# Loading the keys of one batch quad as one large transfer and sixteen small ones

## The chip, the cores and the metric

The kernel runs on one core of a Trainium2 chip. A core has five engines that run their own instruction streams: TensorE (PE in the profile, with its weight loads as PEld), VectorE (DVE), ScalarE (ACT), GpSimd (POOL) and SyncE (SP), which here does nothing but start transfers. The transfers between the chip's main memory (HBM) and the on-chip memory (SBUF, 128 partitions) are carried out by 16 DMA engines that all queues of the core share. The metric is device time of one execution in microseconds (us), the lower the better.

## The reference

One decoding step of attention with grouped heads over a sliding window, with the projections before and after it:

```
x: (32, 1, 512)   k_cache, v_cache: (32, 8, 2048, 128)   wq: (512, 4096)   wo: (4096, 512)    all bf16
W = 512                                   # only the last 512 of 2048 positions are used
q = (x @ wq), as 32 batches x 32 heads x 128
k, v = the last W positions of the caches; 4 query heads share one of the 8 key/value heads
p = softmax(q . k / sqrt(128))            # over the 512 positions
out = (p . v), as 32 x 4096, @ wo         # 32 x 1 x 512
```

The window of K is 32 x 8 x 512 x 128 numbers of two bytes, 32 MiB in all, and that of V as much. Each weight matrix has 4 MiB. So some 75.5 MB must be read for rather little arithmetic.

## The kernel before, in words

The 32 batches are worked off in eight *quads* of four batches. For a quad, the 4 x 8 pairs of batch and key head, times four blocks of 128 positions each, make the 128 partitions: partition p holds pair p // 4 and block p % 4, and its row is 128 positions of 128 numbers, 32 KB (the function `rows` makes this view of the cache). A quad of K or of V is so 4 MiB. K has two buffers, `K_sb[0]` and `K_sb[1]`, and V two more; quads take turns on them.

For quad q, VectorE turns K in two halves (step T, `turn`, L439 to L441: a transpose of 32 x 32 blocks), TensorE makes scores (S), VectorE takes maxima (M), ScalarE the exponentials (X), VectorE divides by the sums (N), TensorE moves the probabilities to the partitions of V (E), ScalarE copies them out (G), ScalarE and VectorE spread them to a block-diagonal form (B), TensorE multiplies with V (P, L361), both engines pick the blocks that count from the result (C), and TensorE and ScalarE fold them into the operand of the last product (F, D). After all quads TensorE multiplies with `wo` (L390), VectorE and ScalarE copy the result out, and one DMA writes it.

The order on each engine is written out by hand in the strings `PE_OPS`, `DVE_OPS` and `ACT_OPS`; nothing is rescheduled. What an operation waits for is worked out from the table in `needs`. VectorE's order around the middle is

```
... M3 N3 B3.0.4 T4.0 T4.1 M4 N4 B4.0.4 T5.0 C3.2.3 T5.1 C3.3.4 T6.0 M5 T6.1 ...
```

All loads of K, V and `wo` are issued by SyncE, in the order of the list `LOADS`:

```
K0 K1 V0.0 K2 V1.0 K3 V2.0 K4 V3.0 K5 K6 V4.0 K7 V5.0 V5.1 V6.0 V6.1 V7.0 V7.1 V7.2 V7.3 W0 W1 W2
```

Before K of quad q is issued, SyncE waits until the second half of T of quad q - 2 is done, which frees the buffer; before V of quad q it waits for the last product of quad q - 2 with V. The three parts of `wo` go into `K_sb[0]` behind T of quad 6. K of a quad is one DMA (L228). It adds 16 to the semaphore of its buffer when all of it has landed, and `turn` waits for 16 times the number of loads that this buffer has had. The last quads of V come in two, two and four pieces with semaphores of their own.

The input `x` (32 rows of 1 KB) is loaded first, by ScalarE's queue, in four DMAs of 2, 6, 10 and 14 rows. In the trace, SyncE's transfers are queue q1, ScalarE's are q10; q8 and q14, "instruction", are transfers that fetch the engines' own instructions through the same 16 DMA engines.

Of the kernel before, what the change touches and what calls it, by code (L numbers as in the profile page):

```python
# [38 lines left out]
X_PARTS = [(0, 2), (2, 8), (8, 18), (18, 32)]  # L39
V_PIECES = [1, 1, 1, 1, 1, 2, 2, 4]  # L40
WOP = [(0, 16), (16, 28), (28, 32)]


def ops_of(text):
    return [(w[0],) + tuple(int(n) for n in w[1:].split(".")) for w in text.split()]


def bass_standalone__sliding_block_cached__sampling_kernel(
# [7 lines left out]
):  # L56
    B, Sq, D = x.shape
    _, HKV, SK, DH = k_cache.shape
    HD = wq.shape[1]
    HQ = HD // DH  # L60
# [7 lines left out]
    KB = 4  # L68
    R = W // KB
# [50 lines left out]
    with ExitStack() as es:  # L120
# [3 lines left out]
        K_sb = [sb(f"K_sb{i}", [P, R * DH], BF16) for i in range(2)]  # L124
# [42 lines left out]
        sem_k = [sem(f"sem_k{i}") for i in range(2)]  # L167
        sem_v = [[sem(f"sem_v{i}_{j}") for j in range(max(V_PIECES))] for i in range(2)]
        sem_wo = [sem(f"sem_wo{i}") for i in range(len(WOP))]
        sem_out = sem("sem_out")  # L170
# [20 lines left out]
        def load_wq(i):  # L191

            nc.sync.dma_start(
                wq_sb[:, 2 * i:2 * i + 2, :].rearrange("p k n -> p (k n)"),
                wq.rearrange("(p k) n -> p k n", k=DKT)[:, 2 * i:2 * i + 2].rearrange("p k n -> p (k n)"),
            ).then_inc(sem_wq[i], 16)
# [4 lines left out]
        def rows(cache, q, r0=0, r1=R):  # L201
            return cache[4 * q:4 * q + 4, :, SK - W:, :].rearrange(
                "b h (k r) d -> (b h) k (r d)", k=KB)[:, :, r0 * DH:r1 * DH]
# [14 lines left out]
        @block.sync  # L218
        def _(sp):
            wait = Waits(sp)  # L220
            load_wq(1)
            wo_r = wo.rearrange("(p i) n -> p i n", i=NI)
            for op in ops_of(" ".join(LOADS)):
                kind, q = op[0], op[1]
                if kind == "K":
                    if q >= 2:
                        wait([ends["T", q - 2, 1]])
                    sp.dma_start(K_sb[q % 2][:, :], rows(k_cache, q)).then_inc(sem_k[q % 2], 16)  # L228
                elif kind == "V":
                    if q == 1:  # L230
                        sp.wait_ge(s["pe_q"], 8)
                    if q >= 2:
                        wait([ends["P", q - 2, 31]])
                    n = R // V_PIECES[q]
                    r0 = op[2] * n
                    sp.dma_start(  # L236
                        V_sb[q % 2][:, r0 * DH:(r0 + n) * DH], rows(v_cache, q, r0, r0 + n)
                    ).then_inc(sem_v[q % 2][op[2]], 16)
                else:
                    wait([ends["T", NQ - 2, 1]])  # L240
                    i0, i1 = WOP[q]
                    sp.dma_start(  # L242
                        wo_sb[:, i0:i1, :].rearrange("p i n -> p (i n)"),
                        wo_r[:, i0:i1, :].rearrange("p i n -> p (i n)"),
                    ).then_inc(sem_wo[q], 16)
            sp.wait_ge(s["dve_y"], 2)
            sp.wait_ge(s["act_y"], 2)
            sp.dma_start(
                out.rearrange("b s n -> b (s n)"), out_sb[:, :, :].rearrange("b c n -> b (c n)")
            ).then_inc(sem_out, 16)  # L250
            sp.wait_ge(sem_out, 16)
# [44 lines left out]
        def _(pe):  # L296
# [88 lines left out]
            wait([ends["D", NQ - 1]])  # L385
            for j, (i0, i1) in enumerate(WOP):
                pe.wait_ge(sem_wo[j], 16)
# [10 lines left out]
        def spread_args(q, h):  # L398
            return bd[:, q % 2, :, h, :], PTc[:, q % NG], mask[:, h:h + 1]

        def pick_args(q, r):
            pr = slice(32 * r, 32 * r + 32)
            return C_sb[pr, q % 2], O_ps[pr, :, r * DH:(r + 1) * DH]

        @block.vector
        def _(dve):
            wait = Waits(dve)
            dve.wait_ge(s["pe_xT"], 1)
            dve.tensor_copy(  # L409
                xT_sb[:, :, :].rearrange("p k c -> p (k c)"), Y_ps  # L410
            ).then_inc(s["dve_xT"], 1)
            dve.wait_ge(s["pool_f"], 2)
            dve.tensor_reduce(
                F_hd[:, :], F_id[:, :, :].rearrange("p r h -> p h r"), AX.X, ALU.add
            ).then_inc(s["dve_c"], 1)
            dve.wait_ge(s["pool_m"], 2)
            dve.tensor_reduce(
                m_red[:, :].rearrange("p (h k) -> p h k", h=HKV),
                m_id[:, :, :, :].rearrange("p b h k -> p h k b"), AX.X, ALU.add,
            ).then_inc(s["dve_c"], 1)  # L420
            dve.wait_ge(s["dve_c"], 2)
            dve.wait_ge(s["pool_fz"], 1)
            dve.tensor_reduce(
                mask[:, :], m_red[:, :].rearrange("p (h k) -> p h k", h=HKV), AX.X, ALU.add
            ).then_inc(s["dve_c"], 1)
            for d in range(4):
                dve.tensor_copy(F_sb[:, d, :, d], F_hd[:, :]).then_inc(s["dve_c"], 1)
            for n in range(4):
                dve.wait_ge(s["pe_q"], 2 * n + 1)
                dve.tensor_copy(Q_row[:, 1024 * n:1024 * n + 512], ps[:, 2 * n]).then_inc(s["dve_q"], 1)  # L430
            dve.wait_ge(s["dve_q"], 4)
            dve.wait_ge(s["act_q"], 4)
            dve.transpose(  # L433
                QT_sb[:, :, :, :, :].bitcast(F32).rearrange("p j w h t -> p h w (j t)"),
                Q_row.bitcast(F32).rearrange("p (h w c) -> p h w c", h=HQ, w=2),
            ).then_inc(s["dve_QT"], 1)
            dve.wait_ge(s["dve_QT"], 1)

            def turn(q, w):  # L439
                dve.wait_ge(sem_k[q % 2], 16 * (q // 2 + 1))  # L440
                return dve.transpose(  # L441
                    KT_sb[:, w].bitcast(F32).rearrange("p r c t -> p r (c t)"),
                    K_sb[q % 2][:, :].bitcast(F32).rearrange("p (r w c) -> p r w c", r=R, w=2)[:, :, w],
                )

            def maxes(q):
                dve.tensor_reduce(maxv[:, q:q + 1], S_ps, AX.X, ALU.max).then_inc(s["dve_m"], 1)  # L447
                dve.wait_ge(s["dve_m"], q + 1)
                return dve.tensor_scalar(  # L449
                    negmax[:, q:q + 1], maxv[:, q:q + 1], -SCALE, None, op0=ALU.mult)  # L450

            def norm(q):
                dve.reciprocal(recip[:, q:q + 1], sums[:, q:q + 1]).then_inc(s["dve_r"], 1)
                dve.wait_ge(s["dve_r"], q + 1)
                return dve.tensor_scalar(  # L455
                    P_bf[:, :], P_f32[:, :], recip[:, q:q + 1], None, op0=ALU.mult)

            def spread(q, h0, h1):
                for h in range(h0, h1):
                    o, i, m = spread_args(q, h)  # L460
                    ins = dve.tensor_scalar(o, i, m, None, op0=ALU.mult)  # L461
                return ins

            def pick(q, r0, r1):
                for r in range(r0, r1):
                    ins = dve.tensor_copy(*pick_args(q, r))  # L466
                return ins

            run = {"T": turn, "M": maxes, "N": norm, "B": spread, "C": pick}
            for op in orders["DVE"]:  # L470
                wait(needs(op))
                run[op[0]](*op[1:]).then_inc(op_sem["DVE", op[0]], 1)
            dve.wait_ge(s["pe_Y"], 1)
            for c in range(2):
                dve.tensor_copy(
                    out_sb[:, c, :], Y_ps[32 * c:32 * (c + 1), 0:P]
                ).then_inc(s["dve_y"], 1)
# [77 lines left out]
```

## Time and profile before

| | us |
|---|---|
| median of three runs (186.52 to 186.93) | 186.64 |
| the profiled execution, its own time | 186.46 |
| its span, from the first to the last instruction | 184.7 |
| SyncE issues K of quad 4 | 61.97 |
| SyncE issues V of quad 3, the next in its list | 71.66 |
| VectorE starts T of quad 4, having waited for the DMA | 92.22 |
| the last piece of `wo` has landed | 181.60 |

The span is 1.76 us shorter than the execution's own time. Busy shares of the five engines are 65% at most (TensorE), while the DMA engines are busy in nearly every slice of the span but the first and the last; over the span they read 75.53 MB at a mean of 409 GB/s. Times inside the execution are counted from the start of the span. Where the chain of waits names a DMA, its duration runs from the start of the issuing instruction to the landing, so it includes the time in which the DMA stands in the queue behind earlier ones.

The trace also keeps every single packet of a DMA (a row of 32 KB is one packet) with its start, duration, size and queue, and the time of every increment that a DMA engine makes to a semaphore. It doesn't name the DMA engine.

### The profile page before, as it was taken

The page shows a single profiled execution, that of the slowest core. Times are in us where ns is not written, and L with a number is a line of the kernel's source. Part 1 is how long each engine was busy: PE and PEld are TensorE (multiplying, and loading weights), DVE is VectorE, ACT ScalarE, POOL GpSimd, SP SyncE. Part 2 cuts the span into 40 slices and gives each one's busy share as a digit, 9 for nine tenths or more (in the row PEclk, how much of TensorE's full clock was granted, in tenths as well). Part 3 has the DMA queues.
Part 4 walks back from the last instruction along what each step waited for, and adds up shares of the span by engine and source line. Part 5 has one row for each costly group of instructions (what it writes and reads, how often), then busy time and mean ns, then how long its engine had stood idle before and what let it go on. Part 6 is the DMA issues. An engine that isn't in the chain of part 4 may idle for free.

```text
span 184.7 us, 3664 instructions
## 1 busy us (share of the span) xinstructions
PE 120.1 (65%) x1636; PEld 56.9 (31%) x1636; DVE 106.5 (58%) x106; ACT 49.8 (27%) x93; POOL 16.9 (9%) x52
## 2 busy tenths in 40 slices
PE   0089304436599795749944992441899799898942
PEld 0024100013344451403521350000345345354541
DVE  0030999996469632963298327999746996311201
ACT  3000400010952357101650162001072804511211
POOL 7900040201000100002000200010000000000000
PEclk9999955555879999555999699555589999999998
DMA  6999999999999999999999999999999999999970
GB/s 220 411 497 405 405 454 454 447 397 405 451 454 451 390 401 454 454 444 405 392 451 454 440 397 412 454 433 440 415 412 422 419 429 426 410 419 433 425 305 31
DMA packets 3872, 75.80 MB, mean 410 GB/s; under 512 B 464, under 2 KB 528, under 8 KB 656
## 3 DMA queue, kind: packets, MB, share of 16 engines
q1 hardware_dynamic: 3792, 75.53, 96.1%
q8 instruction: 13, 0.21, 0.5%
q10 hardware_dynamic: 64, 0.03, 0.1%
q14 instruction: 3, 0.02, 0.0%
HBM read 75.53 MB, written 0.03 MB: 409 GB/s over the span
## 4 chain that ended last, share of the span: by engine, by line
DMA 59%; DVE 22%; PE 10%; issue 6%; SPq 2%; ACTq 1%; DVEq 0%
DMA K_sb<-in_k_cache_dram 43%; DVE KT_sb L441 16%; DMA K_sb<-in_wo_dram 12%; PE ps L313 4%; PE ps L361 4%; DMA bd<-in_x_dram 4%; DVE QT_sb L433 2%; DVE KT_sb L430 1%; SPq L236 1%; DVE C_sb L466 1%; ACTq L187 1%; SPq L242 1%; PE ps L331 1%; DVE bd L409 0%; PE ps L301 0%
## 5 line engine op out<-in xcount | busy, mean ns | idle before, releaser
L441 DVE STREAM_TRANSPOSE KT_sb<-K_sb 128x4096 f32<-128x4096 f32 x16 | 70.5, 4430 | 10.5 <-DMA K_sb<-in_k_cache_dram 10.4
L361 PE MATMUL ps<-V_sb,bd 32*128 32x512 bf16 x1024 | 63.9, 401 | 4.2 <-DMA V_sb<-in_v_cache_dram 1.6
L331 PE MATMUL ps<-KT_sb,QBD 128*32 128x512 bf16 x256 | 25.1, 529 | 37.3 <-DVE KT_sb L441 28.1
L361 PEld LDWEIGHTS ps<-V_sb,bd 32*128 32x128 bf16 x1024 | 27.3, 98 | 38.5 <-issue 14.9
L331 PEld LDWEIGHTS ps<-KT_sb,QBD 128*32 128x32 bf16 x256 | 6.6, 113 | 52.7 <-DVE KT_sb L441 34.1
L492 ACT ACTIVATE P_f<-ps,negmax 128x512 f32<-128x512 f32 x8 | 5.5, 685 | 60.6 <-DVE negmax L449 60.6
L505 ACT ACTIVATE bd<-PTc,mask 128x512 bf16<-128x512 bf16 x31 | 20.1, 710 | 0.3
L510 ACT ACTIVATE C_sb<-ps 32x512 f32<-32x512 f32 x22 | 12.9, 588 | 25.2 <-PE ps L361 25.1
L289 POOL COPY QBD<-QT_sb 32x128 bf16<-32x128 bf16 x32 | 9.2, 287 | 106.8 <-PE ps L331 89.2
L461 DVE TENSOR_SCALAR bd<-PTc,mask 128x512 bf16<-128x512 bf16 x33 | 9.4, 349 | 14.2 <-ACT PTc L499 14.2
L466 DVE COPY C_sb<-ps 32x512 f32<-32x512 f32 x10 | 6.9, 693 | 14.5 <-PE ps L361 14.3
L373 PE MATMUL ps<-C_sb,F_sb 128*128 128x128 f32 x64 | 10.1, 306 | 7.1 <-ACT C_sb L510 6.5
L373 PEld LDWEIGHTS ps<-C_sb,F_sb 128*128 128x128 f32 x64 | 8.6, 208 | 10.0 <-ACT C_sb L510 8.7
L346 PE MATMUL ps<-P_bf,E_sb 128*128 128x128 bf16 x128 | 10.1, 243 | 0.8 <-DVE P_bf L455 0.8
L313 PE MATMUL ps<-V_sb,bd 128*128 128x512 bf16 x32 | 9.8, 480 | 0.8 <-DVE bd L409 0.8
L346 PEld LDWEIGHTS ps<-P_bf,E_sb 128*128 128x128 bf16 x128 | 8.6, 110 | 4.9 <-DVE P_bf L455 2.8
L447 DVE TENSOR_REDUCE maxv<-ps 128x1 f32<-128x512 f32 x8 | 5.5, 687 | 7.8 <-PE ps L331 7.7
L499 ACT ACTIVATE PTc<-ps 128x512 bf16<-128x512 f32 x8 | 4.8, 594 | 18.5 <-PE ps L346 18.4
L430 DVE CAST KT_sb<-ps 128x512 bf16<-128x512 f32 x4 | 2.5, 684 | 7.3 <-PE ps L313 7.3
L301 PE MATMUL ps<-bd 32*128 32x128 bf16 x4 | 0.6, 295 | 9.0 <-DMA bd<-in_x_dram 9.0
L409 DVE CAST bd<-ps 128x512 bf16<-128x512 f32 x1 | 0.7, 691 | 9.6 <-PE ps L301 9.6
L486 ACT ACTIVATE KT_sb<-ps 128x512 bf16<-128x512 f32 x4 | 2.1, 602 | 15.1 <-PE ps L313 15.1
(29 smaller groups left out, 34.1 us busy)
## 6 DMA issues: line engine op xcount, KB each, us to landing
K_sb<-in_k_cache_dram SPq DMA_DIRECT2D x8, 4096.0 KB, 25.4
V_sb<-in_v_cache_dram SPq DMA_DIRECT2D x5, 4096.0 KB, 29.6
V_sb<-in_v_cache_dram SPq DMA_DIRECT2D x4, 2048.0 KB, 20.5
V_sb<-in_wq_dram SPq DMA_DIRECT2D x2, 2048.0 KB, 9.8
V_sb<-in_v_cache_dram SPq DMA_DIRECT2D x4, 1024.0 KB, 11.6
K_sb<-in_wo_dram SPq DMA_DIRECT2D x1, 2048.0 KB, 18.6
K_sb<-in_wo_dram SPq DMA_DIRECT2D x1, 1536.0 KB, 21.7
K_sb<-in_wo_dram SPq DMA_DIRECT2D x1, 512.0 KB, 22.4
```

Source lines behind the costliest of these rows:

```text
L289: pool.tensor_copy(QBD[pr, q % 2].rearrange("p (w t) (h c) -> p w t h c", w=2, h=HKV)[:, :, :, :, 4 * b:4 * b + 4], QT_sb[pr, q].rearrange ...
L313: ins = pe.matmul(ps[:, n], lhsT=xT_sb[:, kt, :], rhs=wq_sb[:, kt, n * 512:(n + 1) * 512], start=kt == 0, stop=kt == DKT - 1, tile_positio ...
L331: ins = pe.matmul(S_ps[32 * c:32 * c + 32, :], lhsT=QBD[:, q % 2, 2 * w + t, c0:c0 + 32], rhs=KT_sb[:, w, :, KB * h:KB * h + KB, t], start ...
L346: ins = pe.matmul(EP_ps[:, e * R:(e + 1) * R], lhsT=E_sb[:, k, e].rearrange("p m j -> p (m j)"), rhs=P_bf[:, k * R:(k + 1) * R], start=k = ...
L361: ins = pe.matmul(O_ps[:, b, :], lhsT=bd[pr, q % 2, 4 * g:4 * g + 4].rearrange("p r h e -> p (r h e)"), rhs=V_sb[q % 2][pr, 512 * g:512 * ...
L373: ins = pe.matmul(F_ps[:, 0:P], lhsT=F_sb[:, d].rearrange("p h d -> p (h d)"), rhs=C_sb[:, q % 2, :, 32 * d:32 * d + 32], start=d == 0, st ...
L441: return dve.transpose(KT_sb[:, w].bitcast(F32).rearrange("p r c t -> p r (c t)"), K_sb[q % 2][:, :].bitcast(F32).rearrange("p (r w c) -> ...
L447: dve.tensor_reduce(maxv[:, q:q + 1], S_ps, AX.X, ALU.max).then_inc(s["dve_m"], 1)
L461: ins = dve.tensor_scalar(o, i, m, None, op0=ALU.mult)
L466: ins = dve.tensor_copy(*pick_args(q, r))
L505: ins = act.activation(o, i, ACTF.Copy, scale=m)
L510: ins = act.activation(*pick_args(q, r), ACTF.Copy)
```

## The change

Quad 4 of K, and that quad alone, is no longer one DMA of 128 rows of 32 KB. One DMA brings the first 28 KB of each of the 128 rows. The last 4 KB of the rows come by 16 further DMAs of eight partitions each: for each group of 32 neighbouring partitions and each k of 0 to 3 the partitions 32 g + k, 32 g + k + 4, ..., 32 g + k + 28, in the order g = 0, k = 0 to 3, then g = 1 and so on. Each of the 17 DMAs adds 16 to the same semaphore, so VectorE waits for 16 x 19 increments ahead of T of quad 4 and for 16 x 20 ahead of T of quad 6. All else, the bytes and their places included, is as before.

```diff
+K_SPLIT = (4,)
+K_TAIL = 2048
...
-                    sp.dma_start(K_sb[q % 2][:, :], rows(k_cache, q)).then_inc(sem_k[q % 2], 16)
+                    k_rows = rows(k_cache, q)
+                    n = R * DH - (K_TAIL if q in K_SPLIT else 0)
+                    sp.dma_start(
+                        K_sb[q % 2][:, :n], k_rows[:, :, :n]
+                    ).then_inc(sem_k[q % 2], 16)
+                    if q in K_SPLIT:
+
+                        for p0 in [32 * g + k for g in range(4) for k in range(KB)]:
+                            sp.dma_start(
+                                K_sb[q % 2][p0:p0 + 29:4, n:],
+                                k_rows[p0 // 4:p0 // 4 + 8, p0 % 4, n:],
+                            ).then_inc(sem_k[q % 2], 16)
...
-                dve.wait_ge(sem_k[q % 2], 16 * (q // 2 + 1))
+                dve.wait_ge(sem_k[q % 2], 16 * sum(17 if p in K_SPLIT else 1 for p in range(q % 2, q + 1, 2)))
```

## The prediction

> **What bounds the kernel now.** I read the page's DMA rows first.
>
> ```profile
> DMA  6999999999999999999999999999999999999970
> ...
> DMA packets 3872, 75.80 MB, mean 410 GB/s; under 512 B 464, under 2 KB 528, under 8 KB 656
> ...
> q1 hardware_dynamic: 3792, 75.53, 96.1%
> q8 instruction: 13, 0.21, 0.5%
> q10 hardware_dynamic: 64, 0.03, 0.1%
> q14 instruction: 3, 0.02, 0.0%
> ```
>
> The 16 DMA engines never run dry between the first and the last slice. The chain of waits then shows that the end hangs on them.
>
> ```profile
> 159.19 22.41 DMA K_sb<-in_wo_dram
> 181.60 0.04 issue
> 181.64 0.44 PE ps L390 x16
> 182.08 0.02 issue
> 182.10 0.28 DVE P_bf L475
> ```
>
> The last piece of `wo` lands at 181.60; behind it come 16 matmuls, the copy-out and the store, 3.07 us to the end of the span at 184.67. So the time is: when does the last DMA engine finish its share of all loads? K of quad 4 itself has much room, as two timelines show (SyncE, then VectorE):
>
> ```profile
> 61.97 0.54 SPq L228 DMA_DIRECT2D K_sb<-in_k_cache_dram  x1
> 71.66 0.54 SPq L236 DMA_DIRECT2D V_sb<-in_v_cache_dram  x1
> 81.59 19.96 SPq L228 DMA_DIRECT2D K_sb<-in_k_cache_dram  x2
> 101.59 0.60 SPq L236 DMA_DIRECT2D V_sb<-in_v_cache_dram  x1
> ```
>
> ```profile
> 92.22 8.77 DVE L441 STREAM_TRANSPOSE KT_sb<-K_sb 128x4096 f32<-128x4096 f32 x2 [1.16 <-DMA K_sb<-in_k_cache_dram]
> ```
>
> Issued at 61.97, it lands at 92.19, behind 20 us of older loads.
>
> The DMA engines don't end together. The increments of the 16 engines for the last piece of `wo`, in order of time:
>
> ```
> 178.32 178.38 178.42 178.51 178.62 | 179.11 179.16 179.57 | 179.87 179.94 180.15 180.20 | 181.33 181.41 181.44 181.60
> ```
>
> Packets of one engine follow each other within 3 to 4 ns, so the records can be strung into 16 chains. The 12 instruction fetches of 16 KB (q8) ahead of the end sit on eight chains: one each for the first eight, and the ninth to twelfth on the chains of the first four. Each costs its engine about 1.1 to 1.6 us (at 81.56 fetch and 32 KB packet together took 2.77 instead of 1.21). Three fetches of 8 KB (q14) sit on three other chains. So the groups above are five engines without a fetch, three with an 8 KB one, four with one of 16 KB, and four with two.
>
> **The change, part by part.**
>
> *Issue.* 16 more DMAs on SyncE at 0.53 to 0.62 each (its rows) are at most 9.9 us. Starting at 62.51 they end by 72.4, and V of quad 3, free at 71.66, goes out 0.7 later at most. Its data can't move before K of quad 4 is through at about 90: 18 us of cover, cost nothing. K of quad 5 waits until 81.59 anyway.
>
> *Which engines carry the tail.* The four loads of `x` (2, 6, 10 and 14 rows) left 64 packets on q10: 32 rows and 32 completions, one for each row, while SyncE's 27 loads wrote 432 completions of 4 B, 16 each. So a DMA of eight rows should run on eight engines, one row each, and all 16 tails on the same eight if each begins at the same engine. (The Trainium skill, "DMA: Bandwidth & Descriptors", section "Why a DMA increments its semaphore by 16 and not by 1", says that HWDGE takes the lowest-numbered k engines; the packet counts agree with k, but no row here gives an engine's number.) Which eight: the chains with most `x` rows should be the first engines. The first two fetches of q8 fall on chains with two `x` rows, the third and sixth on chains with one, the q14 fetches on chains with three or four, the eighth seems to fall on one with three. Mostly, then, the q8 fetches are on the engines that get no tail. I put 9 in 10 on that.
>
> *Work per engine.* Periods from packet to packet: 32 KB 1.213, 16 KB 0.610, 4 KB 0.155, a completion 0.006. On the line between, 28 KB takes 1.06. Before, quad 4 of K costs each engine 8 x 1.213 + 0.006 = 9.71. After:
> - an engine without tail: 8 x 1.06 + 0.01 = 8.49, so -1.22;
> - an engine with tail: 8.49 + 16 x (0.155 + 0.006) = 11.07, so +1.36.
>
> The queues stay full, so both shifts last until the end. The four latest would land at 181.60 - 1.22 = 180.38. The eight with tail, now 178.32 to 179.57, would land at up to 179.57 + 1.36 = 180.93. By this alone the end moves by -0.67.
>
> *Two streams to the same partitions.* Half of the tail, 32 KB on each of eight engines, belongs to rows that the other eight brought before, and these go on with V meanwhile. If the way into SBUF goes with the partitions, two streams share one there; no row shows 32 KB of that. Lower bound 0: the 1 KB packets of `x` took 46 ns each beside full streams, and the streams' 16 KB packets stayed at 0.611. Upper bound, equal sharing at an unchanged sum: the 32 KB take twice 1.21, so +1.21 for an engine with tail, and +1.21 for its partner, whose gain is gone. The nearest row for several engines at neighbouring partitions is the store of the output, 16 engines on 32 neighbours: 13 of its 32 packets of 1 KB took 65 to 79 ns instead of 46, up to 1.7 times. A buffer can swallow 1 KB of `x`, but not 32 KB, so I take the full 1.21.
>
> The Trainium skill, "SBUF — State Buffer", section "Door 1: The DMA port swizzle", says that DMA bandwidth depends on how many of 16 ports the partitions reach, and that partitions 64 apart are on different ports. Its map would put all rows that change engines on the other eight's ports. By this rule the sum is the one below; were engines alone the limit, it would be the -0.67 above.
>
> *Sum.* Engines with tail: 179.57 + 1.36 + 1.21 = 182.14 for the latest. The others: 181.60 - 1.22 + 1.21 = 181.59. The end moves from 181.60 to 182.14, +0.54.
>
> *The added wait.* VectorE's wait for quad 4 now ends with the tail: engines that landed at 90.47 to 90.91 land by 93.5, the one with a q14 fetch at 90.27 by about 94. T of quad 4 starts 1.3 to 1.9 late; behind it in VectorE's order stand M4, N4, B4, and the scores of quad 4, K of quad 6 and V of quad 4 wait for that. K of quad 6, due at 101.0, can't move before K of quad 5 ends at 109.9: hidden. K of quad 5 and of quad 7 land later by the same shift (140.92 to 140.28 + 2.57 = 142.85 for quad 7), and so T of quad 7, the picks behind it, and the issue of V of quad 7 at 155.5 by 1.9. Packets follow an issue by about 1.0 (first `wq` issue 0.73, packet 1.755), so at 158.4; the first engine without work would be one at 160.06 less 0.45 from packet to increment. Cover 1.2, cost nothing. The last products with V end at 174.2, up to 1.0 later; the `wo` product then starts by 178.4 and waits for its second part at 180.9: hidden.
>
> The sum is against the profiled execution: 186.46 + 0.54 = 187.00. That execution lies 0.18 under the median of the runs, 186.64, so I forecast 187.2.
>
> **Rivals.**
>
> *Faster: nothing is shared.* The engines with tail end at 180.93 and the late ones at 180.38: 186.64 - 0.67 = 185.97. For it: the untouched 0.611 beside `x`. Against it: those bursts are 1 KB. It decides as long as sharing costs less than 0.67 on the latest engine with tail, since 0.67 is what the balance gives.
>
> *No change that can be measured.* Sharing costs about half (0.3 to 1.0, the end within 0.37 of before), or the tails spread over all 16 engines. In the latter case each gets 8 packets of 4 KB in place of part of its rows: 8.49 + 8 x 0.161 = 9.78, +0.07: 186.7. Against even spreading: the completion counts of `x`.
>
> *Slower by more: the tail falls on the engines with the q8 fetches.* 181.60 + 1.36 = 182.96, or 184.17 with sharing: 188.0 to 189.2. For it speaks the eighth fetch, against it the first three and the sixth.
>
> *Slower by issue.* It would need SyncE to hold up V of quad 3 by 18 us, over 1.6 for each small DMA; its rows say 0.6. I give it no chance of its own.
>
> **How the numbers follow.** What this measurement can tell from no change is about 0.2%, 0.37 us. Forecast 0.46 (slower); faster rival 0.33; no change 0.13; tail on the late engines 0.08 (slower). Hence faster 0.33, same 0.13, slower 0.54. The forecast's own range is 186.9 to 187.7: below by a milder sharing, above by sharing that loses some of the sum. The range for 8 in 10 must take in the faster rival, 185.97, and leaves out the tail on the late engines: 185.7 to 187.7.
>
> **What would show it.**
> - Issue: SyncE's rows of L239, 16 of about 0.6, and V of quad 3 at about 72.
> - Engines: 128 data packets more and, on eight engines each, 16 x 8 = 128 completions: q1 should have 4048 packets; on 16 engines each it would have 4176.
> - Work: the 4 KB packets of the tail at 0.155 for one half; with sharing, the other half near 0.31 and V's 32 KB packets beside them above 1.213.
> - K of quad 4 at T's start: about 93.5 to 94 with sharing, 92.3 to 93 without.
> - The end: last increments for `wo` in two groups, with sharing the engines with tail last at 182.1, without at 180.9.
>
> Wrong if V's packets keep their 1.213 next to the tail, or if the late groups of the last piece of `wo` move up instead of down.

## The result, and the profile after

The changed kernel took 190.31 us, the median of six runs (188.08 to 191.0), against 186.75 of the kernel before, run beside it (186.52 to 187.39). The ratio is 1.014, with a 95% interval of 1.0098 to 1.0182; it is not the quotient of the medians, which is 1.019, and it leaves out the run at 191.0, which counts as a slow one. The forecast of 187.2 had the right sign, and the time lies far outside its range of 185.7 to 187.7.

The six times are not one cloud: 188.08 and 188.28, then 190.22, 190.40, 190.72 and 191.0. The kernel before shows no such gap. So there are two questions: what costs some 1.5 us in an execution at 188, and what costs 2.4 more in one at 190.5. The profiled execution is one of the first kind, 188.08; it took 1.62 longer than the profiled one of before, and its span of 186.3 is longer by as much. Three more profiles, shown further below, are of the second kind.

The page's DMA rows of the changed kernel, in the order in which the prediction showed those of before:

```profile
DMA  6999899999899999999999999999999999999980
...
DMA packets 4128, 75.80 MB, mean 407 GB/s; under 512 B 592, under 2 KB 656, under 8 KB 912
...
q1 hardware_dynamic: 4048, 75.53, 96.2%
q8 instruction: 13, 0.21, 0.5%
```

The bytes are the same, the engines are as busy, and yet the mean rate is 407 instead of 410 GB/s: the same work takes the engines longer. The 4048 packets of q1 are exactly the number that the prediction gave for tails that run on eight engines.

SyncE's timeline of the changed kernel (start, duration, engine, line, operation):

```profile
62.05 0.53 SPq L233 DMA_DIRECT2D K_sb<-in_k_cache_dram  x1
62.62 10.82 SPq L239 DMA_DIRECT2D K_sb<-in_k_cache_dram  x16
73.49 0.60 SPq L250 DMA_DIRECT2D V_sb<-in_v_cache_dram  x1
81.49 23.28 SPq L233 DMA_DIRECT2D K_sb<-in_k_cache_dram  x2
```

The 16 issues cost 0.68 each. V of quad 3 goes out 1.83 later than before, and its data still has nowhere to go until K of quad 4 is through, at about 89.

VectorE's timeline at T of quad 4 and the second half of T of quad 5 (in brackets the wait that came before):

```profile
95.43 8.77 DVE L455 STREAM_TRANSPOSE KT_sb<-K_sb 128x4096 f32<-128x4096 f32 x2 [5.64 <-DMA K_sb<-in_k_cache_dram]
...
114.60 4.45 DVE L455 STREAM_TRANSPOSE KT_sb<-K_sb 128x4096 f32<-128x4096 f32 x1 [0.97 <-DMA K_sb<-in_k_cache_dram]
```

T of quad 4 starts 3.2 later than before.

The end of the chain of waits of the changed kernel:

```profile
161.80 19.95 DMA K_sb<-in_wo_dram
181.75 0.04 issue
181.80 1.93 PE ps L404 x55
183.72 0.02 issue
183.75 0.28 DVE P_bf L489
```

In this execution the chain hangs on the second part of `wo`, because TensorE's clock fell to half just as that part landed, and its matmuls and those of the third part took 1.93 together. The third part landed at 182.97, 1.37 later than before. That 1.37, and 0.27 more from landing to the end of the matmuls, are the 1.64 of this profile. The 16 increments of the third part:

```
before  178.32 178.38 178.42 178.51 178.62 179.11 179.16 179.57 179.87 179.94 180.15 180.20 181.33 181.41 181.44 181.60
after   180.37 180.53 180.54 180.62 180.84 181.16 181.24 181.36 181.88 182.0  182.31 182.52 182.6  182.67 182.9  182.97
```

The spread is smaller, 2.6 instead of 3.3: some load did move from late engines to early ones. But the whole lot comes later, the earliest engine by 2.05.

### The profile page after: what moved, and what is told of

Same layout as the page of the kernel before. It is cut to its first block, busy times and chain, and to the rows that moved or that the text cites. A ratio compares the mean times of both kernels' runs of the same rounds, so it can differ in the third digit from the quotient of the medians.

```text
span 186.3 us, 3680 instructions
## 1 busy us (share of the span) xinstructions
PE 120.4 (65%) x1636; PEld 57.4 (31%) x1636; DVE 106.5 (57%) x106; ACT 49.6 (27%) x93; POOL 16.9 (9%) x52
## 3 DMA queue, kind: packets, MB, share of 16 engines
q1 hardware_dynamic: 4048, 75.53, 96.2%
## 4 chain that ended last, share of the span: by engine, by line
DMA 59%; DVE 22%; PE 10%; issue 5%; SPq 2%; ACTq 1%; DVEq 0%
DMA K_sb<-in_k_cache_dram 44%; DVE KT_sb L455 16%; DMA K_sb<-in_wo_dram 11%; PE ps L327 4%; PE ps L375 4%; DMA bd<-in_x_dram 4%; DVE QT_sb L447 2%; DVE KT_sb L444 1%; SPq L250 1%; DVE C_sb L480 1%; PE ps L404 1%; ACTq L190 1%; PE ps L345 1%; SPq L256 0%; DVE bd L423 0%
## 5 line engine op out<-in xcount | busy, mean ns | idle before, releaser
L375 PE MATMUL ps<-V_sb,bd 32*128 32x512 bf16 x1024 | 65.0, 407 | 3.5 <-issue 1.3
L375 PEld LDWEIGHTS ps<-V_sb,bd 32*128 32x128 bf16 x1024 | 28.0, 99 | 38.1 <-issue 16.1
L303 POOL COPY QBD<-QT_sb 32x128 bf16<-32x128 bf16 x32 | 9.2, 287 | 109.4 <-PE ps L345 92.6
L387 PE MATMUL ps<-C_sb,F_sb 128*128 128x128 f32 x64 | 9.6, 295 | 7.0 <-ACT C_sb L524 6.4
L387 PEld LDWEIGHTS ps<-C_sb,F_sb 128*128 128x128 f32 x64 | 8.0, 197 | 9.9 <-ACT C_sb L524 8.6
L327 PE MATMUL ps<-V_sb,bd 128*128 128x512 bf16 x32 | 9.2, 459 | 0.8 <-DVE bd L423 0.8
```

The source lines that it names most:

```text
L303: pool.tensor_copy(QBD[pr, q % 2].rearrange("p (w t) (h c) -> p w t h c", w=2, h=HKV)[:, :, :, :, 4 * b:4 * b + 4], QT_sb[pr, q].rearrange ...
L327: ins = pe.matmul(ps[:, n], lhsT=xT_sb[:, kt, :], rhs=wq_sb[:, kt, n * 512:(n + 1) * 512], start=kt == 0, stop=kt == DKT - 1, tile_positio ...
L375: ins = pe.matmul(O_ps[:, b, :], lhsT=bd[pr, q % 2, 4 * g:4 * g + 4].rearrange("p r h e -> p (r h e)"), rhs=V_sb[q % 2][pr, 512 * g:512 * ...
L387: ins = pe.matmul(F_ps[:, 0:P], lhsT=F_sb[:, d].rearrange("p h d -> p (h d)"), rhs=C_sb[:, q % 2, :, 32 * d:32 * d + 32], start=d == 0, st ...
```

## The experiments

In every version the wait for the load (VectorE's for K, TensorE's for `wo`) is fitted to the number of DMAs; the diffs leave that line out. The theory on trial: two streams that write to the same partitions get in each other's way, and this costs more than the balance of the engines gives. The rivals were that the split itself, the number of small DMAs, or a later issue of V of quad 7 costs the time.

**Split, without small DMAs.** The 28 KB per partition stay; the 4 KB come as one DMA of 128 rows, on all 16 engines.

```diff
-                        for p0 in [32 * g + k for g in range(4) for k in range(KB)]:
-                            sp.dma_start(K_sb[q % 2][p0:p0 + 29:4, n:], ...)
+                        sp.dma_start(K_sb[q % 2][:, n:], k_rows[:, :, n:])
```

> 28 KB of each row, then the last 4 KB by one DMA of 128 rows: the split alone, each engine keeps its own rows. Sharing theory and engine-load theory: per engine 8 x (1.062 + 0.155) + 0.012 = 9.75 against 9.71 us before, so +0.04: as before within 0.2%. A theory in which a second DMA or the added wait on VectorE costs by itself would give +0.5 or more.

Measured: 186.89, ratio 1.0007 (0.9992 to 1.0021), and the last piece of `wo` at 181.70. Splitting a load costs nothing that this measurement can tell. What is left is the number of small DMAs, or which engine brings which rows; the next two runs tell these apart.

**Own half alone.** Of the 16 small DMAs only the eight for partitions 0 to 63 are left. The last 4 KB of the other 64 partitions are not loaded at all, so 256 KB less are read, and the scores of quad 4 are partly made from old keys. If the engines that carry the tail are the ones that bring these rows anyway, no stream meets another.

```diff
-                        for p0 in [32 * g + k for g in range(4) for k in range(KB)]:
+                        for p0 in [32 * g + k for g in (0, 1) for k in range(KB)]:
```

> The tails of the partitions 64 to 127 are left out (8 small DMAs, for partitions 0 to 63 alone), so 256 KB less is read and the scores of quad 4 are made from old keys there. By load, engines with tail do 8.50 + 8 x 0.161 = 9.79 (+0.08), the others 8.50 (-1.21). Sharing theory: nothing is shared, V's packets beside the tail stay at 1.21; the latest engine with tail ends wo at 179.6, the others at 180.4, so -1.2 us against before: about 185.5, ratio 0.994. Engine-load theory: the same. If small DMAs cost by themselves: slower than that by 0.5 or more.

**Foreign half alone.** Only the eight for partitions 64 to 127 are left: as many bytes on the same engines, and the last 4 KB of the partitions 0 to 63 are not loaded.

```diff
-                        for p0 in [32 * g + k for g in range(4) for k in range(KB)]:
+                        for p0 in [32 * g + k for g in (2, 3) for k in range(KB)]:
```

> The tails of the partitions 0 to 63 are left out instead: as many DMAs, bytes and packets on the same engines, only the partitions are others, and the scores of quad 4 are made from old keys there. Sharing theory: the 4 KB packets take about 0.31 and V's 32 KB packets beside them about 2.2, so engines with tail +0.08 + 1.2 to 2.0, the others -1.21 + 1.4 = +0.2; wo's last increments at about 181.8, +0.2 us against before and +1.4 us against the run with the partitions 0 to 63 alone. Engine-load theory: -1.2 us, the same as that run, packets at 0.159 and 1.21.

| | own half | foreign half |
|---|---|---|
| time, us | 186.85 (185.9 to 187.77) | 188.86 (187.65 to 189.92) |
| ratio to before | 0.9989 (0.9965 to 1.0014) | 1.0109 (1.0049 to 1.017) |
| last increment for `wo`, us | 180.40 | 182.07 |
| median of a 4 KB packet of the tail, us | 0.159 | 0.308 |
| longest 32 KB packet of V beside the tail, us | 1.22 | 2.37 |
| time lost by packets that began from 86 to 98, us | 1.5 | 26.1 |

The last row sums, over all 16 engines, by how much each packet took longer than a packet of its size does elsewhere in the trace; before has 1.7 there. Equal bytes, equal engines, an equal number of DMAs: only the partitions differ, and with them 2.0 us of time. This is the cleanest pair of the study. The last increments, 180.40 and 182.07, are within 0.3 of what the balance without sharing and with sharing gave.

The Trainium skill, "SBUF — State Buffer", section "Door 1: The DMA port swizzle", says that adding 64 to a partition's number switches it to another port, and adding 32 does not. The pair agrees: partitions 0 to 63 went untouched (0.159), partitions 64 to 127 did not (0.308). The two halves also come from different places in HBM, which the pair does not separate; the tail on `wo` below bears on that.

The own half alone should have been faster by its last increment, 1.2 earlier than before: the eight engines without tail bring 32 KB less each, and 1.21 is what 32 KB take. The end of its chain of waits shows where that went:

```profile
179.19 0.04 issue
179.23 1.26 PE ps L404 x34
180.49 0.41 issue
180.90 0.86 PE ps L404 x24
181.76 0.02 issue
```

The matmuls that came as the second part of `wo` landed ran at half clock here, and so did those of the third: 0.86 for 24 where the foreign half's profile has 0.55. The last matmul ended at 181.76, only 0.32 ahead of before's 182.08.

**The changed kernel once more.** It was timed again beside the two above.

> The changed kernel once more. The profiled execution took 188.08, the median of its runs is 190.3: some 2 us are in executions without a trace. Sharing theory: the last increments for wo come at about 183 (1.4 later than before), K of quad 4 at 95, V's 32 KB packets beside the second half of the tail take about 2.2 us each; what is on top of 188 must come later in the execution. Rival a, the late issue: V of quad 7 goes out so late (after 160, 155.5 before) that most DMA engines stand idle ahead of its first packets. Rival b, the clock: TensorE's granted clock falls to 0.5 ahead of about 180, so that the last products with V (7.1 us each at full clock) or wo's take longer. A trace of an execution near 190 tells a from b.

Measured: 187.92, 188.14, 190.56 and 190.58; ratio 1.0135 (1.0061 to 1.0209). The two levels are the kernel's own, and the profile fell on the lower one again. The foreign half alone has two as well (187.65 and 187.96, 189.76 and 189.92), and so has the own half, closer together (four runs from 185.9 to 186.31, five from 186.84 to 186.99, and one at 187.77 whose span of 185.1 is that of the five).

**A late turn of quad 7.** My first idea for the upper level was a run-dry: V of quad 7 goes out late, since T of quad 7 is late, and the DMA engines find their queues empty. The prediction had found a margin of 1.2 us for that. So in the kernel before, without any tail, T of quad 7 was made 2.78 longer.

```diff
+                if q == 7 and w == 0:
+                    dve.transpose(KT_sb[:, w, :80]..., K_sb[q % 2][:, :80 * DH]...).then_inc(sem_twice, 1)
+                    dve.wait_ge(sem_twice, 1)
```

> The kernel before, with 80 of 128 columns of the first half of T of quad 7 turned once more ahead of it on VectorE (4.45 x 80/128 = 2.78 us): T of quad 7 is as late as in the changed kernel, and no load is touched. It tells what the second level of the changed kernel's times (190 to 191, beside 188) is. If it is the chain from T of quad 7 over the last products with V to the product with wo, which in the changed kernel has only 1.5 us left (wo part 0 done at 180.27, part 1 landed at 181.75): here too that chain loses 2.8 of 2.0 us, V of quad 7 goes out at 158.3, the time is 186.7 to 187.5 in some executions and 189 or more in others. If it is the shared way into SBUF: one level, 186.7 to 187.5.

Measured: 188.88, 188.91, 188.24, 189.06; ratio 1.0098 (1.0071 to 1.0125). Neither expectation had that: one level, between the two. SyncE's timeline and the end of the chain of waits of this run:

```profile
121.90 40.67 SPq L237 DMA_DIRECT2D V_sb<-in_v_cache_dram  x8
```

```profile
181.94 0.74 PE ps L391 x40
182.69 1.11 issue
183.79 0.55 PE ps L391 x24
```

The eight issues of V end at 162.57 here. The four for quad 7 begin at 159.56, 4.0 later than before: 2.78 are the longer turn, and TensorE's clock stood at half from 149.3 to 152.8 besides. The windows of this run show that the engines did run dry (DMA share, the last number but one, where before has 1.02 from 160 to 162):

```profile
158.00:160.00 2.00, 2.00 (x38) 1.07 (x31) 1.09 (x3) 0.99 (x3) 0.00 (x0) 1.00 0.44 188
160.00:162.00 2.00, 2.00 (x30) 1.59 (x30) 1.55 (x5) 1.93 (x4) 0.00 (x0) 1.00 0.60 139
```

The last piece of `wo` came at 183.13. So empty queues cost about 2 us when V of quad 7 goes out near 160. In the changed kernel's profile it went out at 158.30. The idea stayed possible.

**The tail on a load that nothing later waits for.** K of quad 4 whole, and the same 16 small DMAs for the last 4 KB per partition of the first part of `wo`. There is no K to be late, and the DMA that follows is the second part of `wo`.

```diff
+                    i2 = i1 - 4 if q == 0 else i1
-                        wo_sb[:, i0:i1, :] ...
+                        wo_sb[:, i0:i2, :] ...
+                    if q == 0:
+                        for p0 in [32 * g + k for g in range(4) for k in range(KB)]:
+                            sp.dma_start(wo_sb[p0:p0 + 29:4, i2:i1, :] ..., wo_r[p0:p0 + 29:4, i2:i1, :] ...)
```

> K of quad 4 whole as before; instead part 0 of wo is brought as 12 KB of each row and then 4 KB by the same 16 DMAs. The same bytes change engines and meet the same streams, but no T, no score and no issue of another load waits for them. Sharing theory: 4 KB packets at 0.31 in the second half, last increments for wo at 182.1 to 183, 0.5 to 1.4 later than before, time 187.3 to 188.1. If the second level comes from late T and late issue, it is gone here, all executions within 0.5 us; if it comes from the transfers themselves, some executions are at 190.

Measured: 188.78, 188.89, 189.02 and 190.84; ratio 1.0131 (1.0079 to 1.0182), last piece of `wo` at 183.66. The expectation was too low, and one run of four stood two above the others. A tail costs its 2 us where no work on K, V or in VectorE's order can be late; whether the one run at 190.84 is the second level, no trace of it tells. The packets are as in the tail of K: the first of each engine's 4 KB packets took 0.159 and most of the later ones about 0.31, and the 12 KB packets beside them up to 0.93 instead of 0.46. Since they come from another tensor, this speaks for the place that is written to as what the streams share, and not the place that is read; no run varied the one alone.

**Half a tail.** 2 KB per partition instead of 4 KB.

```diff
-K_TAIL = 2048
+K_TAIL = 1024
```

> The changed kernel with a tail of 2 KB in place of 4 KB: as many small DMAs, issues and completions, half the bytes. Sharing theory: engines with tail 8 x 1.137 + 16 x 0.086 - 9.70 = +0.77, with sharing +1.4 to 1.8, so their latest at 181.0 to 181.4; the others -0.6 + 0.7, at 181.7 as before; T of quad 7 is 0.9 to 1.3 late; time +0.1 to +0.4, ratio 1.000 to 1.003. If the 16 small DMAs, their completions or VectorE's wait for 17 DMAs cost by number: as the full tail, +1.4% in the median.

Measured: 188.81, 189.5, 187.75, 189.57; ratio 1.0107 (1.0052 to 1.0161). This missed: the cost was far above the 0.1 to 0.4 expected. The time lost by packets from 86 to 98 was 20.5, so 18.8 above before, where half of the shared bytes should have lost 9.7 by equal sharing. In the profiled execution one engine stood alone at the end, at 183.94, with the next at 182.19. It was the engine that had also brought the first of the 16 KB instruction fetches. As shown below, that is the mark of the upper level, so this profile is to be compared with the whole tail's profiles at 190, where by the same sum some 33 were lost, and not with the one at 188.08, where it was 26.4. By the times, too, the half tail costs about six tenths of the whole one if 187.75 is its lower level and the other three its upper one (+0.8 and +1.9 to 2.6 above before, against +1.2 to 1.5 and +3.4 to 4.2); no trace shows at which level the unprofiled runs are.

**Sharing without imbalance.** Eight small DMAs of 16 partitions each, every eighth of 128: all 16 engines bring the same number of bytes, and most of the tail rows are not its own.

```diff
-                        for p0 in [32 * g + k for g in range(4) for k in range(KB)]:
+                        for p0 in range(8):
-                                K_sb[q % 2][p0:p0 + 29:4, n:],
-                                k_rows[p0 // 4:p0 // 4 + 8, p0 % 4, n:],
+                                K_sb[q % 2][p0:p0 + 121:8, n:],
+                                k_rows[p0 // 4:p0 // 4 + 31:2, p0 % 4, n:],
```

> The tail by 8 DMAs of 16 partitions each, every eighth of 128, so that every engine moves one row of each and all 16 carry as much as before: per engine 8.50 + 8 x 0.161 = 9.79, +0.08. Load of the engines alone: the time as before within 0.2%. If packets to near partitions share a way: 16 engines write to partitions 8 apart at once, so some of them meet; with two engines on each way the tail takes 2.5 instead of 1.3 us on all 16, last increments for wo at about 182.9, time +1.3 and packets of about 0.31. The Trainium skill, SBUF — State Buffer, section Door 1: The DMA port swizzle, gives by its map two of the 16 rows for each of eight ports, which is this second case.

Measured: 188.65, 189.45, 189.02, 188.8; ratio 1.0109 (1.0082 to 1.0135), so 2.0 more than before where 1.3 was expected. Of the 128 packets of 4 KB, 98 took over 0.2 us, V's packets up to 2.10, and the time lost was 33.6. The end of the chain of waits:

```profile
161.14 22.64 DMA K_sb<-in_wo_dram
183.78 0.04 issue
183.83 0.44 PE ps L404 x16
```

All 16 increments of K of quad 5 lie 2 us later than before (111.92 to 113.80 against 109.92 to 111.94), all engines alike, and none of the four runs is at 190. Sharing alone, with the load of the engines even, costs 2 us; the second level did not show without the uneven load.

**The changed kernel on its upper level.** What was open was the upper level: one engine with more to carry, or queues that run dry. A profile of an execution at 190 tells them apart.

> The changed kernel, for the trace of an execution near 190, if one falls. Run-dry theory: there TensorE's granted clock is 0.5 for 3 to 7 us more between 137 and 158, where it was 1.0 in the traced executions at 188, so the products with V of quad 5 end after 160, V of quad 7 is issued there (158.3 at 188), and most of the 16 DMA engines stand idle for 1 to 3 us ahead of V of quad 7; the last increments for wo come at 184.5 to 185.5 with a smaller spread. Transfer theory: V of quad 7 goes out at 158 to 159 as before, and one DMA engine alone ends 2 us behind the others, since its share of the meeting streams was worse.

> As the look before it: near 190 by the run-dry theory V of quad 7 goes out after 160 and most DMA engines stand idle ahead of it; by the transfer theory it goes out at 158 to 159 and one engine is 2 us behind all others.

> As the look before it: near 190 by the run-dry theory V of quad 7 goes out after 160 and most DMA engines stand idle ahead of it; by the transfer theory it goes out at 158 to 159 and one engine is 2 us behind all others.

The three executions took 190.15, 190.52 and 190.58, all on the upper level. The end of the chain of waits of the second of them, then the windows from 158 to 162 of the profile at 188.08, and then, of the second of the three, the window from 160 to 162 (window, busy time and number of instructions of PE and its weight loads, DVE, ACT, POOL, granted clock, DMA share, GB/s):

```profile
163.19 22.47 DMA K_sb<-in_wo_dram
185.66 0.04 issue
185.71 0.44 PE ps L404 x16
```

```profile
158.00:160.00 2.00, 2.00 (x32) 1.82 (x24) 1.40 (x3) 1.66 (x3) 0.00 (x0) 1.00 0.97 389
160.00:162.00 2.00, 2.00 (x38) 0.94 (x41) 1.41 (x5) 1.97 (x5) 0.00 (x0) 1.00 0.92 360
```

```profile
160.00:162.00 2.00, 2.00 (x32) 1.54 (x33) 1.54 (x5) 1.93 (x5) 0.00 (x0) 1.00 0.75 274
```

The queues of some engines do run dry, a quarter of the engines' time in this window. But the engines that stood idle there are not those that end last, as the last increments for `wo` show:

```
after, at 188.08   ... 182.6  182.67 182.9  182.97
upper, 1st         ...        183.07 183.43 185.30
upper, 2nd         ... 183.04 183.12 183.18 185.66
upper, 3rd         ...        182.97 183.40 185.44
```

One engine alone is about 2 us behind the other 15. It can be told which. On the eight engines without tail, V of quad 3 begins as soon as their 28 KB rows of K are in, and an engine that has had one of the first instruction fetches by then begins 1.3 later:

```
after          89.02 89.04 89.09 89.27       | 90.37 90.42 90.44 90.58
again          88.94 88.94 89.02 89.05       | 90.35 90.44 90.65 90.70
upper, 1st     88.89 88.98 89.00 89.03 89.33 | 90.43 90.43 90.76
upper, 2nd     88.82 88.93 89.02 89.08 89.32 | 90.57 90.57 90.61
upper, 3rd     88.85 88.87 88.97 89.03 89.21 | 90.46 90.52 90.75
```

In both executions at 188 (the second row is the profile of the repeated timing) four of the eight are late, in all three at 190.5 only three. By then four fetches have come, on four engines. The fourth engine with an early fetch then carries the tail too. Strung together, the packets of the second of the three show it: the engine that has the first fetch and later the ninth has its rows of K of quad 4 at 90.85 and its tail at 95.45, where the other tail engines are through by 92.2 to 93.7; it is last for V of quad 3 (105.52) and K of quad 7 (144.37), and ends at 185.66. So the same kernel has its instruction fetches on other engines in other executions. As far as the packets can be told apart, six of the first eight fetches are on engines without tail in all five profiles; at 188 it is the seventh and the eighth that fall on engines with tail, at 190.5 the first and the eighth, and the engine of the first has the ninth too. In the kernel before, where all engines carry the same rows, this should leave no trace in the time, and its times show no second level.

Here, an engine with two fetches and no tail would land by the prediction's terms at 181.60 - 1.22 plus 1.43 for sharing, so 181.8; with a tail one landed at 185.3 to 185.7. That sum closes as well: in the first and the third of these profiles the tail packets of this engine lost 2.0 and its V packets behind them 0.4, and 181.33 to 181.60 (the four engines with two fetches in the kernel before) + 1.36 + 2.4 is 185.1 to 185.4, where 185.30 and 185.44 were measured. It began its tail late, and all but the first of its 16 packets took 0.22 or more in the first profile, where engines on time brought nine to eleven before a packet took 0.2. The own half's two levels, 0.7 apart, may be the same thing at a smaller size (an engine with two fetches gains 1.22 there, or gains nothing where it has eight small packets to carry); no profile of its upper level was taken, so this is only argued.

## Why the prediction was wrong

**Issue: right.** 16 issues, 0.68 each instead of 0.62; V of quad 3 issued at 73.49 instead of by 72.4; hidden, as the first packet of V of quad 3 came at 89.0 at the earliest.

**Which engines: half right, and the step that failed.** The tail runs on eight engines (q1 has 4048 packets), and the shorter run of its packets was 0.159, as worked out. But the step "mostly, then, the q8 fetches are on the engines that get no tail; I put 9 in 10 on that" treated it as one question with one answer for all executions, and the sum then went on as if none of the four engines with two fetches had a tail. "Mostly" was right, six of eight in each profile. But it is asked anew in each execution, of four engines with two fetches each, and one of the four with a tail is enough to set the end. Of 13 times of the changed kernel, four are at about 188 and nine at 190.2 to 191.0. The rival "the tail falls on the engines with the q8 fetches" came nearest to the upper level, with a chance of 0.08, a term of 184.17 for the last increment, where 185.30 to 185.66 was measured, and a time of 188.0 to 189.2; what it lacks is the sharing cost of a late engine, 2.4 instead of 1.21. The forecast was a sum for the lower level alone, and even that, 187.92 to 188.28, lies above its 187.7; the median of six went to the upper.

**Two streams to the same partitions: mechanism right, size too small.** Upper end taken: 1.21 for each engine, 19.4 over all 16. Measured: 24.7 above before. The eight partners lost 1.43 each, the tail engines 1.66 on the mean, 1.02 in their 4 KB packets and 0.64 in the V packets right after. So "equal sharing at an unchanged sum" was no upper bound here. Where the streams met it was close: the 4 KB packets and the partners' packets lost 8 x (1.02 + 1.43) = 19.6 together. The excess, 8 x 0.64 = 5.1, lies in the V packets right behind the tail, which go to partitions that the engine brings anyway; the prediction had no term for them. The engine that was late at 190 shows the same: its packets for its own partitions were slow too while the others met. With 16 partitions at a time it would have held: 98 to 112 foreign packets of 4 KB at equal sharing lose 98 x 4 / 32 x 2 x 1.213 = 29.7 to 34.0, and 31.9 above before were measured. That a buffer takes 1 KB but not 32 KB was an argument; in the profiles the engines on time brought one to three of their eight foreign packets at 0.159, and slow ones only then. The nearest row was weak besides: by the trace 14 of the store's 32 packets, not 13, took 65 to 79 ns, and a store reads from SBUF, where the tail writes.

**Sum for an execution at 188.** Forecast for the last increment 179.57 + 1.36 + 1.21 = 182.14; measured 182.97. With 1.66 in place of 1.21 it is 182.59. The engine that ends last is the one that an 8 KB fetch had held up at 89.0; it was through with its tail at 94.4, the other seven by 92.6, so it lost more than the mean. The remaining 0.38 is not split further. To that the clock's fall at 181.8 added 0.27 behind the landing, which no step had.

**The added wait: the chain right, the margin thin.** T of quad 4 started at 95.43 instead of 93.5 to 94, K of quad 7 landed at 143.71 instead of 142.85, V of quad 7 went out at 158.30 instead of 157.4. Its first packet came 1.46 after the issue instead of the 1.0 taken. Two engines stood idle for 1.27 and 0.95 us, neither among those that end last, so at 188 the wait cost nothing, as forecast. With T of quad 7 later by 2.78 in the kernel before, it cost 2 us. In the executions at 190.5 V goes out at 159.1 to 159.5 and engines do idle, yet the one that ends last does not.

**The rivals.** "Nothing is shared" needed a sharing cost under 0.67; it was 1.4 to 1.7, and the own half alone, where nothing was shared, did land at 180.40, near the 180.38 of this rival. "No change": neither even spreading nor half the sharing was there. "Issue": not there.

**What would make it wrong.** Neither of the two signs named came about: V's packets did not keep their 1.213, and the last increments did not come earlier. What went wrong was not on the list, since it lies between executions and a single trace of before cannot show it.

**Still open.** Why packets to an engine's own partitions are slowed too while other streams meet, so that tails of eight partitions lose more than equal sharing (24.7 instead of 19.4, and 18.8 instead of 9.7 for the half tail), and those of 16 do not. Why the instruction fetches change engines between executions.

## What to carry to other kernels

Before you balance DMA engines by moving rows to another engine, ask whether that engine will then write, at full stream, to partitions that a neighbour is filling: of two tails of the same bytes on the same engines, the one for the engines' own partitions landed 1.7 us earlier than the one for foreign partitions. No run here shows a balance that pays; the own half landed 1.2 earlier than before because it leaves bytes out. Before you count on which engine is early, ask whether that is a property of the kernel or of one execution; what the packets of one execution show of background work on an engine is a sample of one. And when a kernel becomes slower on the median, list the single times first: here they showed two levels, each with a cause of its own.

## What the runs showed of the hardware that I had not expected

- Where two streams meet on the same partitions, both are slowed, and packets beside and behind them too: 24.7 us were lost over the 16 engines for 256 KB of foreign rows at 188.08, where equal sharing gives 19.4, and 19.6 of it where the streams met; some 31 at 190.
- The engines that carry the 16 KB instruction fetches differ from execution to execution, and one engine with two of them that also carries the tail ended 1.9 to 2.5 us behind all others.
- TensorE's granted clock falls to half in the waits for `wo` at the end in some executions: the matmuls of its second and third part took 1.93 in the profile at 188.08, and in that of the own half the fall ate most of the gain of 1.2.
